# FFT-form 7x7 convolution on one core: a later gate for the pixel loads, an earlier weight difference, DMA lanes in program order, four output buffers

## The chip, the cores and the metric

The kernel runs on one core of a Trainium2 chip. The metric is the device time of one execution in microseconds (us). Each execution is classed fast or slow (slow here: over 1.5% above the fastest of the same kernel), and only fast ones are compared; one execution, of e11, was slow and is left out. The profile's span is about 1.7 us shorter than the device time of the same execution.

## The reference, cut to what matters

```python
def reference(x, w):                 # x: 1x224x224x96 bf16, w: 7x7x96x96 bf16
    wp = jnp.pad(w, ((0, H - K), (0, W - K), (0, 0), (0, 0)))
    Xf = rfft2(x as f32, axes=(1, 2))
    Wf = rfft2(wp as f32, axes=(0, 1))
    Yf = jnp.einsum('bhwi,hwio->bhwo', Xf, Wf)
    return irfft2(Yf, s=(H, W)) as bf16
```

It is a circular 7x7 convolution with 96 input and 96 output channels.

## The kernel before

The kernel transforms only along the height, in blocks of 28 rows plus 6 of overlap. `Fm` is the forward matrix (pixels to frequencies, written to `xf`), `WF` the filters in the frequency domain, made from `wq` by matmuls and, for about a third of the slots, as a difference of two others (`w_sub`). VectorE forms the combined input `J` (42 operations `J<-J` in the run, one per group of frequencies and tile). The products land in PSUM banks (`pb`), become `yf`, and go through a scratch buffer in HBM (`scr`), from which they come back transposed (`tt`) for the inverse matrix `Gm`. Results are cast to `yo` and stored.

The last tile has no later work to hide behind, so it is stored in four parts, `scra` (frequencies 0 to 8) and three `scrb`, loaded back into `xf` buffers that are free by then, and multiplied in two halves, `GA` and `GB`. Between the halves, 16 filler matmuls on zeros (`wu`) are meant to keep TensorE's clock up.

By the instruction listing every DMA takes one of eight semaphores, called lanes here, in turn, in the order in which the scheduler meets it, and waits for the DMA that had the lane last. The traces show DMAs landing on eight semaphores, and the longest wait of one DMA for another on the sync queue of the kernel before is 6.3 us (for `scrb<-yf`).

```python
    gate = []
    def dma(out_ap, in_ap):                      # loads and stores on the sync queue
        r = DE.dma_start(out=out_ap, in_=in_ap)
        if gate:                                 # held until gate[-1] has run
            tc.add_manual_dep(r.ins, gate[-1].ins.name, SYNC, reason="queue order")
        return r
    ...
    for _ in range(3):                           # warm-up: 3 x 8 matmuls on zeros
        pwu = bank()
        for _ in range(8):
            TE.matmul(pwu[:]..., lhsT=wu[:, 0:128], rhs=wur, start=True, stop=True)
    ...
    xgo = sin_q(qf[:])                           # sine table, ScalarE
    ...
    after(xgo, x0_loads)                         # first pixel loads: J edge rows, then xn
    ...
    VE.tensor_copy(out=Fm.rearrange("p r s j -> p j s r"), in_=qf[:])
    ...
    def put_y(t, s):                             # store of a group of rows of yf
            ...
            def put(eng=DE):
                eng.dma_start(out=dst..., in_=yf[...])
            if t == TL and s < NS - 1:           # last tile: on ScalarE's queue
                puts.append(lambda: put(SE))
            else:
                put()
    ...
    yo_pool = ctx.enter_context(tc.tile_pool(name="yo", bufs=3, side="right"))
    ...
            if s == 3:
                queue_c(t - 1)                   # tt loads of the tile before
            ...
            if t == TL and s == SL[2] + 2:
                load_b(0, DE, 1)                 # first scrb load
    ...
    load_b(1, DE, 1)
    load_b(2, DE, 1)
    ...
    order = [(g, q) for h in range(2) for g in range(2) for q in range(4 * h, 4 * h + 4)]
    live = {k: first(*k) for k in order[:8]}     # GA halves
    for _ in range(WARM):                        # 16 fillers
        TE.matmul(live[order[7]]..., lhsT=wu[:, 0:M4], ...)
    for i, (g, q) in enumerate(order):
        second(g, q, live[(g, q)], yo)           # GB halves, cast, store
```

## Time and profile before

| | before |
|---|---|
| time, three executions | 290.65 us median (290.49 to 291.18) |
| profiled span | 288.5 us |
| TensorE, VectorE, ScalarE, GpSimd busy | 92%, 84%, 64%, 30% |
| GB matmuls start, start to end of the run | 279.06, 9.4 us |

In the profile's lines PE is TensorE, PEld its weight loads, DVE VectorE, ACT ScalarE, POOL GpSimd; SPq and ACTq are DMAs issued on the sync queue and on ScalarE's. The granted clock is the share of TensorE's full clock that the chip's throttle let through. From the page of the kernel before: a row of busy tenths of TensorE in 40 equal slices of the span, and the granted clock in tenths of full speed.

```profile
PE   8398898999989889999999999999999999999592
PEclk9869999999979999999999999999999999999867
```

One digit is 7.2 us. TensorE has its gaps in the second slice (the filters are not there yet) and in the last slices. The clock fell to half at 12.3, 80.6 and 271.7 us, for 6.83, 3.41 and 6.83 us, and once more when the work was done (285.4). In this trace all falls and rises are whole multiples of 3.41 us apart; one such step of 3.41 us, between two places of this grid, is called a window below. From the list of waits of the kernel before (what waited for what; us in total, times, longest):

```profile
ACT yo L82 <- DMA out_dram<-yo: 3.2, 1, 3.2
...
PE pb L82 <- ACT yo L82: 2.3, 1, 2.3
DVE yo L82 <- DMA out_dram<-yo: 2.2, 1, 2.2
```

All three stand in the tail near 272 us.

### The profile page before, as it was taken

What the parts mean: (1) busy time and instruction counts of PE and PEld (TensorE: products, weight loads), DVE (VectorE), ACT (ScalarE), POOL (GpSimd) and SP (SyncE); (2) the same over time, 40 slices, a digit from 0 to 9 for tenths busy, and PEclk for the clock granted to TensorE, in tenths of its full rate; (3) what the DMA queues carried; (4) which work ended last, traced back from release to release, by engine and by line L of the source; (5) the groups of instructions that cost most, each with busy time, mean ns of one, the idle gap of its engine ahead of it and who ended that gap; (6) DMA issues with size and microseconds to landing.
All of it is one profiled execution on the core that took longest, in us unless ns stands there. A gap on an engine that the chain in (4) does not pass through costs nothing.

```text
span 288.5 us, 11546 instructions
## 1 busy us (share of the span) xinstructions
PE 266.1 (92%) x4814; PEld 238.4 (83%) x4814; DVE 243.0 (84%) x524; ACT 184.7 (64%) x459; POOL 87.4 (30%) x122
## 2 busy tenths in 40 slices
PE   8398898999989889999999999999999999999592
PEld 3298898999889888888988988898989898889271
DVE  6289999998998999789968899878987789898623
ACT  5089875657413955986888768886688864173313
POOL 2741001234325312521432224223323324426000
PEclk9869999999979999999999999999999999999867
DMA  8667331111211559979688671986749433684955
GB/s 170 132 188 203 83 104 62 45 43 43 85 45 43 168 176 199 284 206 283 166 203 235 180 253 57 228 224 192 250 134 218 150 106 126 181 236 123 222 151 180
DMA packets 44364, 46.01 MB, mean 159 GB/s; under 512 B 33442, under 2 KB 35054, under 8 KB 44216
## 3 DMA queue, kind: packets, MB, share of 16 engines
q1 hardware_dynamic: 43464, 42.90, 55.3%
q10 hardware_dynamic: 848, 2.37, 3.0%
q8 instruction: 38, 0.62, 0.9%
q14 instruction: 14, 0.11, 0.1%
HBM read 23.92 MB, written 21.33 MB: 157 GB/s over the span
## 4 chain that ended last, share of the span: by engine, by line
PE 52%; DVE 29%; DMA 10%; issue 4%; POOL 2%; ACT 1%; DVEq 0%; SPq 0%; POOLq 0%; ACTq 0%
PE pb L82 52%; DVE J L82 9%; DVE v L82 6%; DVE xf L82 5%; DMA wq<-in_w_dram 4%; DVE yf L82 4%; DMA xn<-in_x_dram 4%; DVE WF L82 3%; DVE u L82 2%; DMA out_dram<-yo 2%; POOL yf L82 2%; ACT xf L82 1%; ACT yo L82 0%; DVE tt L82 0%; DVE yo L82 0%
## 5 line engine op out<-in xcount | busy, mean ns | idle before, releaser
L82 PE MATMUL pb<-WF,J 96*128 96x96 bf16 x2898 | 167.6, 207 | 4.4 <-DVE J L82 3.9
L82 PEld LDWEIGHTS <-J 96*128 96x128 bf16 (+1 forms) x2910 | 143.5, 98 | 19.0 <-issue 8.2
L82 POOL TENSOR_TENSOR yf<-v,u 128x384 bf16<-128x384 f32 x75 | 75.3, 1018 | 163.6 <-issue 91.2
L82 ACT CAST xf<-pb 96x408 bf16<-96x408 f32 (+1 forms) x139 | 60.7, 472 | 7.4 <-PE pb L82 4.5
L82 PE MATMUL pb<-WF,xf 96*128 96x96 bf16 x952 | 60.7, 207 | 1.9 <-DVE WF L82 1.8
L82 ACT CAST yo<-pb 84x384 bf16<-84x384 f32 (+1 forms) x130 | 56.1, 481 | 9.4 <-PE pb L82 6.1
L82 DVE TENSOR_TENSOR J<-xf 96x1824 bf16<-96x1824 bf16 (+1 forms) x84 | 57.2, 720 | 0.1
L82 PEld LDWEIGHTS <-xf 96*128 96x128 bf16 x952 | 47.5, 98 | 2.2 <-issue 2.0
L82 PE MATMUL pb<-Fm,xn 118*128 118x136 bf16 x448 | 46.2, 223 | 1.6 <-DVE u L82 0.8
L82 PE MATMUL pb<-tt,Gm 102*84 102x384 bf16 (+1 forms) x144 | 35.7, 329 | 1.3 <-DVE yf L82 0.8
L82 ACT CAST WF<-pb 96x480 bf16<-96x480 f32 (+1 forms) x57 | 29.2, 566 | 9.0 <-PE pb L82 8.8
L82 PEld LDWEIGHTS <-xn 118*128 118x128 bf16 x448 | 30.1, 98 | 2.6 <-issue 1.5
L82 PE MATMUL pb<-wq 98*128 98x120 bf16 (+1 forms) x288 | 24.4, 238 | 4.6 <-DMA xn<-in_x_dram 4.6
L82 PEld LDWEIGHTS <-wq 98*128 98x128 bf16 x288 | 21.5, 151 | 5.2 <-issue 5.2
L82 DVE TENSOR_TENSOR J<-J 96x912 bf16<-96x912 bf16 (+1 forms) x42 | 25.0, 595 | 0.0
L82 DVE TENSOR_TENSOR yf<-v,u 128x384 bf16<-128x384 f32 x36 | 20.5, 571 | 1.2
L82 DVE CAST xf<-pb 96x408 bf16<-96x408 f32 (+1 forms) x33 | 15.5, 506 | 0.7 <-PE pb L82 0.6
L82 PEld LDWEIGHTS <-Gm 102*84 102x84 bf16 (+1 forms) x144 | 11.8, 114 | 4.2 <-issue 1.6
L82 PE MATMUL pb<-wu 128*128 128x512 bf16 (+1 forms) x40 | 12.4, 488 | 1.1 <-DVE ct L82 1.1
L82 DVE CAST WF<-pb 96x480 bf16<-96x480 f32 (+1 forms) x15 | 9.1, 614 | 5.0 <-PE pb L82 4.5
L82 PEld LDWEIGHTS <-wu 128*128 128x128 bf16 (+1 forms) x40 | 6.1, 155 | 6.9 <-issue 2.9
L82 DVE COPY xf<-xf 96x816 bf16<-96x816 bf16 x12 | 9.3, 817 | 0.0
(390 smaller groups left out, 216.4 us busy)
## 6 DMA issues: line engine op xcount, KB each, us to landing
xn<-in_x_dram SPq DMA_DIRECT2D x13, 672.0 KB
scr<-yf SPq DMA_DIRECT2D x30, 288.0 KB
tt<-scr SPq DMA_DIRECT2D x24, 288.0 KB
out_dram<-yo SPq DMA_DIRECT2D x24, 252.0 KB
tt<-scr SPq DMA_DIRECT2D x12, 192.0 KB
out_dram<-yo SPq DMA_DIRECT2D x12, 168.0 KB
scr<-yf SPq DMA_DIRECT2D x6, 192.0 KB
scra<-yf ACTq DMA_DIRECT2D x3, 288.0 KB
```

What stands on the lines that cost most here:

```text
L82: r = fn(*a, **k)
```

## The change

The intent, part by part: (1) the pixel loads wait for the cast of `Fm` instead of the sine, so that the filter loads have the DMA engines alone for longer; (2) eight more warm-up matmuls shorten the hole before the filter matmuls; (3) the first weight difference is made whole in round 0; (4) every DMA is put in program order, so that it takes its lane in that order, and the early stores of the last tile go on the sync queue; (5) four output buffers in place of three; (6) finer cuts of the last stores.

```diff
+    dlast = [None]
+    def dorder(r):
+        if dlast[0] is not None:
+            tc.add_manual_dep(r.ins, dlast[0].ins.name, NOSYNC, reason="program order")
+        dlast[0] = r
+        return r
     def dma(out_ap, in_ap):
 ...
-        return r
+        return dorder(r)
 ...
-    for _ in range(3):
+    for _ in range(4):
         pwu = bank()
 ...
-    xgo = sin_q(qf[:])
+    sin_q(qf[:])
 ...
-    after(xgo, x0_loads)
 ...
-    VE.tensor_copy(out=Fm.rearrange("p r s j -> p j s r"), in_=qf[:])
+    xgo = VE.tensor_copy(out=Fm.rearrange("p r s j -> p j s r"), in_=qf[:])
+    after(xgo, x0_loads)
 ...
-                eng.dma_start(out=..., in_=...)
+                dorder(eng.dma_start(out=..., in_=...))
-            if t == TL and s < NS - 1:
+            if t == TL and SA <= s < NS - 1:
                 puts.append(lambda: put(SE))
 ...                                             (the same dorder() in load_b)
-        add(max(0, 2 * b0 - 10), 2 * b0 - 4 if gi > 1 else 2, ...)
-        ... enumerate(... if gi > 1 else ((0, 0), (1, 0))):
+        add(max(0, 2 * b0 - 10), 2 * b0 - 4 if gi > 1 else 1, ...)
+        ... enumerate(... if gi > 1 else ((0, 0), (0, 0))):
 ...
-                now = wsubs.pop((r, t)) + now if r < 2 else now + wsubs.pop((r, t))
+                now = wsubs.pop((r, t)) + now if r < 1 else now + wsubs.pop((r, t))
 ...
-    yo_pool = ctx.enter_context(tc.tile_pool(name="yo", bufs=3, side="right"))
+    yo_pool = ctx.enter_context(tc.tile_pool(name="yo", bufs=4, side="right"))
 ...
-        cut = (1, 3) if i < 4 or i >= 12 else (3,)
+        cut = (1, 3) if i < 4 else (3,) if i < 12 else (1, 2, 3)
```

More of the change, by code (lines that the diff above doesn't have):

```diff
@@ L569, in put @@
             def put(eng=DE):
-                eng.dma_start(out=dst.rearrange("w j s e -> (w j) s e")[:, y0 - yo0:y1 - yo0],
-                              in_=yf[:, 0:y1 - y0].rearrange("p s r m o -> p s (r m o)"))
-            if t == TL and s < NS - 1:
+                dorder(eng.dma_start(out=dst.rearrange("w j s e -> (w j) s e")[:, y0 - yo0:y1 - yo0],
+                              in_=yf[:, 0:y1 - y0].rearrange("p s r m o -> p s (r m o)")))
+            if t == TL and SA <= s < NS - 1:
                 puts.append(lambda: put(SE))
@@ L599, in load_b @@
             w0, w1 = h * TW // nh, (h + 1) * TW // nh
-            eng.dma_start(out=tl_b[KO[i]:KO[i] + KB[i], w0:w1], in_=sb[:, w0:w1])
+            dorder(eng.dma_start(out=tl_b[KO[i]:KO[i] + KB[i], w0:w1], in_=sb[:, w0:w1]))
     def g_parts():
@@ L715 @@
         b0 = PGRP[gi][0]
-        add(max(0, 2 * b0 - 10), 2 * b0 - 4 if gi > 1 else 2, prep_jobs(gi) if gi > 1 else p1)
-        for h, (r, t) in enumerate(((max(b0 - 4, 2), 1), (b0 - 2, 0)) if gi > 1 else ((0, 0), (1, 0))):
+        add(max(0, 2 * b0 - 10), 2 * b0 - 4 if gi > 1 else 1, prep_jobs(gi) if gi > 1 else p1)
+        for h, (r, t) in enumerate(((max(b0 - 4, 2), 1), (b0 - 2, 0)) if gi > 1 else ((0, 0), (0, 0))):
             wsubs.setdefault((r, t if r >= LAG else 0), []).append(w_sub(gi, h))
@@ L841 @@
             live[order[k]] = first(*order[k])
-        cut = (1, 3) if i < 4 or i >= 12 else (3,)
+        cut = (1, 3) if i < 4 else (3,) if i < 12 else (1, 2, 3)
         if q % 4 in cut:
-            q0 = 0 if q % 4 == cut[0] else cut[0] + 1
+            q0 = max([-1] + [c for c in cut if c < q % 4]) + 1
             w0 = TL * 2 * TW + q // 4 * PXC
```

## The prediction

> **What bounds the kernel now.** I read the page first (TensorE busy 92%, VectorE 84%: no engine is free, so look by stage), then the table of five-microsecond stretches, then the chain that ended last, then the timelines of the two stretches where TensorE is not full: the start and the end. From the table of stretches (busy us of PE, PEld, DVE, ACT, POOL, granted clock, DMA share, GB/s):
>
> ```profile
> 20.00:25.00 5.00, 4.93 (x74) 4.45 (x71) 5.00 (x12) 5.00 (x15) 0.00 (x0) 1.00 0.47 125
> 30.00:35.00 5.00, 4.88 (x89) 4.62 (x88) 5.00 (x11) 4.15 (x11) 0.00 (x0) 1.00 0.19 36
> 35.00:40.00 5.00, 3.78 (x69) 3.55 (x67) 4.96 (x11) 3.66 (x10) 0.00 (x0) 1.00 0.34 114
> ...
> 250.00:255.00 5.00, 5.00 (x103) 4.56 (x100) 4.54 (x11) 2.98 (x9) 1.87 (x2) 1.00 0.77 206
> 270.00:275.00 5.00, 2.66 (x10) 1.64 (x10) 1.46 (x3) 0.85 (x2) 0.00 (x0) 0.67 0.85 222
> ```
>
> From about 18.5 to 50 us VectorE has no hole: it is the bound there, even where TensorE stands still (35 to 40). From about 110 to 266 us TensorE is full. From 267 on nobody is full: that is the tail, bound by waits. The chain through the tail, and the sync queue's timeline there:
>
> ```profile
> 266.20 0.23 ACT tt__7217 L82
> 266.44 6.13 DMA out_dram<-yo
> ...
> 272.64 0.48 ACT yo L82
> ...
> 273.17 9.68 PE pb L82 x41
> ```
>
> ```profile
> 259.39 6.96 SPq L82 DMA_DIRECT2D xf<-scra  x2
> 266.44 0.63 SPq L82 DMA_DIRECT2D out_dram<-yo  x1
> 267.12 0.36 SPq L82 DMA_DIRECT2D xf<-scrb  x1
> 268.62 0.34 SPq L82 DMA_DIRECT2D scrb<-yf  x1
> 272.00 3.04 SPq L82 DMA_DIRECT2D xf<-scrb  x2
> ```
>
> The two loads of the last tile's first part (xf<-scra) should go out together at 259.4; the second goes at 266.03. The queue's waits name the cause:
>
> ```profile
> SPq L82 <- DMA scrb<-yf: 6.3, 1, 6.3
> ```
>
> That second load reads nothing of scrb. The instruction listing shows that it waits for a DMA semaphore lane (there are eight, taken in turn) that a later store on ScalarE's queue holds. The output store behind it is late by the same 6 us, so its yo buffer is late, ScalarE's yo cast waits 3.2 us, TensorE gets no bank (2.3 us), and the 16 filler matmuls start at 274.4. They end only at 278.9, when the second halves (GB) start:
>
> ```profile
> 274.40 4.82 PE L82 MATMUL pb<-wu 128*112 128x384 bf16 x16
> 279.06 0.98 PE L82 MATMUL pb<-xf,GB 128*112 128x384 bf16 x5
> ```
>
> In the start, these matter:
>
> ```profile
> 13.14 4.99 PE L82 MATMUL pb<-wq 98*128 98x100 bf16 x56 [4.56 <-DMA xn<-in_x_dram]
> 36.53 0.33 PE L82 MATMUL pb<-WF,xf 96*128 96x96 bf16 x4 [1.21 <-DVE WF L82]
> ```
>
> The first name is wrong: by the listing these matmuls wait for the six filter loads. The second is the wait that the weight-difference move aims at.
>
> [...] falls and rises at 12.3, 19.1, 80.6, 271.7 and 278.5 us are whole multiples of 3.41 us apart. [...] the fall at 80.6 closes a window with one hole of 1.46 us, that at 271.7 one with nine matmuls in it. [...] the store issued at 268.62 stood behind 432 + 168 + 288 KB of earlier sync-queue work and landed only at about 274.7, when the load that needs it was released. [...] Here a 288 KB store with the queue nearly to itself took 257.08 to 259.36, 2.3 us.
>
> **The change part by part.**
>
> *Pixel loads held to the cast of Fm.* The gate moves from the sine's end (7.24 us) to the cast's end (8.62), 1.4 us later. The small J loads (133 KB) compete less with the filters, but on the engines that finish last (data until 12.0 us) they still queue behind the filter rows. J is needed at 17.9, no earlier. I count 0 to 0.3 us, take 0.1.
>
> *Eight more warm-up matmuls.* At 0.213 us each (spacing of the last ones) they end at 8.58 + 8 x 0.213 = 10.3 instead of 8.6; the hole before the filter matmuls shrinks from 4.5 to 2.8 us. With the holes seen to drop the clock (1.46 us in a window) it still falls in most phases of the window, later. A full clock would remove VectorE's hole between 17.94 and 18.51 and start its first cast some 0.2 us sooner, 0.8 at most; at a chance of a quarter 0.2 us.
>
> *First weight difference whole in round 0.* Eight filter matmuls (two banks) move ahead of the first tile-1 forward matmuls, where TensorE waited 0.7 us for pixels anyway, and the second 0.89 us difference moves up one round. TensorE's 1.21 us wait at 36.5 should go. But VectorE is the bound there and runs the same differences; moving one buys nothing by itself. What does buy: the casts split otherwise. Counting the listing to round 5, VectorE loses a 0.64 us filter cast and a 0.43 us short xf cast and gains one of 0.5: 0.57 us less, ScalarE takes them. So 0.6 us.
>
> *Lanes in program order, early scra stores on the sync queue.* The second scra load goes at 259.8 instead of 266.0, the 56-row output at 260.5, both into a DMA system with idle time (0.0 to 0.1 share from 264 to 267). So the ring is nearly free when the last store goes out at 268.62: I give it 2.4 us, to 271.0, and its load 2.8 us (the same load in the kernel before: issued 274.73, its data through by about 276.5, landed by my estimate at 277.5): GB's data at 273.9, in place of 277.5. TensorE: the twelve tail casts on two engines end at 271.5 (six of 0.49 on VectorE from 268.5), the last first-half matmul at 271.6, then 16 fillers: 2.6 us at full clock (0.163 each), end 274.4; at half clock about 4.3, end 275.9, as the clock comes back within the row. GB starts at 274.4 or 275.9 in place of 278.9: 4.5 or 3.0 us, mean 3.7. Against it: the store of rows 0 to 2 now stands in program order before the tt loads, which start at 247.1 instead of 245.06 (its wait is for GpSimd's yf, end 246.72). The first tile is used at 250.02; with the store's 288 KB ahead in the ring it lands at 250 to 251. TensorE is the bound there: a new wait of 0 to 1 us, take 0.5.
>
> *Four output buffers.* The only waits on yo's stores are the two in the tail (3.2 and 2.2 us). The lane order cures the same wait, so I count nothing extra.
>
> *Last stores cut finer.* One store more of 0.32 us issue, the last one 84 instead of 168 KB; but 688 KB are still to move after 284, at about 290 GB/s. 0.1 us either way: 0.
>
> Sum: 0.1 + 0.2 + 0.6 + 3.7 - 0.5 = 4.1 us. 290.65 - 4.1 = 286.5.
>
> **The rivals.** (a) *The filler takes the DMA's place.* If the clock falls near 271.7 again, the 16 fillers, not the transfer, set GB's start. For it: the tail casts still leave about 1 us of holes in that window. Against: no 2.3 us stop any more. It makes 287.2 instead of 285.7. (b) *The late tt loads stop TensorE at 250.* For it: 2.0 us later issue, 5 us of lead before; against: only the first of six tiles is urgent. At worst 1 us more: 287.5. (c) *The start gives more than I count*: filters land earlier and the clock stays up, VectorE's row starts 1 us sooner; with a full tail gain 284 to 284.5. For it: the author tuned exactly these; against: the DMA engines' late ones are busy with filter rows until 12 us in both. (d) *The start gives nothing*, because another VectorE wait opens behind the doubled difference (it now waits for ScalarE's filter casts): 287.2.
>
> **Range and chances.** Faster by over 2% means under about 284.9: it needs the upper end of both gains. The tail's sum alone is between 2 and 4.7 us, the start's between 0 and 1.6. I predict 286.3 (the sum, a little towards rival c), 283.8 to 288.6; faster 0.2, same 0.79, slower 0.01.
>
> **What would show it.** Right: in the sync queue's timeline both scra loads within 1 us of each other; no yo wait on out_dram; the last scrb load issued about 2.4 us after its store, not 6; the GB matmuls starting about 6 us after that store's issue, in place of 10.3; VectorE without holes from 18 to 50 us, its first combined J at 44.5 coming some 0.6 to 1 us sooner. Wrong: TensorE waiting on tt<-scr near 250 for over 1 us; fillers at 0.3 us each up to the GB matmuls; the filter matmuls starting well before 13.1; or scrb1's store, which shares the engines with scrb0's load, landing later than 270 and holding the queue.

## The result, and the profile after

In four executions each, the changed kernel took 286.35 us (median, 285.81 to 287.81) and the kernel before 290.91 us (290.49 to 291.51): ratio 0.985, 95% interval 0.981 to 0.989, within 2%. Here and below a ratio is the mean time of one kernel's fast runs over that of the other's of the same rounds, so not quite the ratio of the medians that are quoted.

That first reading agrees with the prediction to 0.05 us, better than it deserves. Later (e5), in six executions, the same kernel took 288.41 us (287.14 to 289.36) and the kernel before 290.99: ratio 0.992 (0.989 to 0.995). Over all ten executions the median is 287.5 us, and eight of the ten lie in the predicted range. Much of what the experiments found is about where this spread comes from.

From the page of the changed kernel, the same two rows (7.1 us a digit), in the execution of 285.95 us:

```profile
PE   8599998999979889999999999999999999989982
PEclk9979999999979999999999999999999999999998
```

The gap in the tail is gone and the clock stays up there. Two of its five-microsecond stretches (busy us of PE, PEld, DVE, ACT, POOL, granted clock, DMA share, GB/s), to be laid beside those of the prediction:

```profile
35.00:40.00 5.00, 4.73 (x87) 4.35 (x85) 4.96 (x11) 4.58 (x12) 0.00 (x0) 1.00 0.28 95
...
270.00:275.00 5.00, 3.69 (x21) 2.45 (x21) 0.78 (x2) 0.00 (x0) 0.00 (x0) 1.00 0.72 189
```

At 35 to 40 us TensorE works 4.73 instead of 3.78 us, and VectorE has no hole in either kernel (4.96): the wait has gone, the bound has not moved. At 270 to 275 the clock is 1.00 instead of 0.67. The sync queue's timeline of the changed kernel (start us, us, queue, what):

```profile
245.19 0.35 SPq L82 DMA_DIRECT2D scra<-yf  x1
245.72 4.32 SPq L82 DMA_DIRECT2D tt<-scr  x9
...
259.56 0.99 SPq L82 DMA_DIRECT2D xf<-scra  x2
...
268.03 0.34 SPq L82 DMA_DIRECT2D scrb<-yf  x1
268.55 3.77 SPq L82 DMA_DIRECT2D xf<-scrb  x2
```

Both scra loads go within a microsecond, the lane wait is gone. The last scrb load leaves at the end of the last row, 272.0 us, 4.0 us after its store: the prediction gave the store 2.4. TensorE's timeline of the changed kernel, with the idle time before a group in brackets:

```profile
249.73 0.49 PE L82 MATMUL pb<-tt,Gm 102*84 102x384 bf16 x2 [1.09 <-DMA tt<-scr]
...
271.00 2.76 PE L82 MATMUL pb<-wu 128*112 128x384 bf16 x16
274.79 0.99 PE L82 MATMUL pb<-xf,GB 128*112 128x384 bf16 x5 [1.03 <-issue]
```

The new wait for tt is there (1.09 us). The fillers run at full clock and end at 273.76, and GB then waits another microsecond for the last load: the profile names no releaser here, but the trace's semaphore of that load is complete at 274.70. GB starts 6.8 us after the last store's issue; before it was 10.4.

**A ledger.** To find where the time went I subtracted the start times of the same `J<-J` operation in two profiles. All differences are to the profile of the kernel before, in us; negative is earlier. The first J stands at 27.46 us there, the others at the times in the header, GB at 279.06; the last columns are the time from the last J to GB, and the span.

| profile | 1st J | 37.7 | 181.6 | 253.6 | 258.8 | last J, 263.0 | GB | last J to GB | span |
|---|---|---|---|---|---|---|---|---|---|
| before | 0 | 0 | 0 | 0 | 0 | 0 | 0 | 16.04 | 288.5 |
| changed kernel, first | -0.03 | -0.45 | -0.74 | -1.54 | -1.02 | -0.64 | -4.27 | 12.41 | 284.2 |
| changed kernel, again (e5) | +0.52 | +0.09 | +0.06 | -0.72 | +1.46 | +1.85 | -2.75 | 11.44 | 285.5 |
| head alone (e1) | +0.94 | +0.52 | +0.55 | +0.59 | +0.85 | +1.24 | +1.64 | 16.44 | 290.0 |
| tail alone (e2) | -0.12 | -0.12 | -0.04 | -0.84 | -0.40 | -0.01 | -3.05 | 13.00 | 285.4 |
| four buffers (e3) | +0.25 | +0.25 | +0.34 | -0.45 | -0.45 | -0.07 | -2.38 | 13.73 | 286.2 |
| lanes in order (e4b) | -0.33 | -0.33 | -0.26 | +3.39 | +3.39 | +3.68 | +1.48 | 13.84 | 291.4 |
| lanes and scra stores (e6) | +0.36 | +0.35 | +0.34 | +0.35 | +4.05 | +4.44 | -0.25 | 11.35 | 288.2 |
| tt loads first (e7) | +0.57 | +0.14 | +0.26 | -0.54 | -0.55 | -0.16 | -3.89 | 12.31 | 284.7 |
| six warm-up rows (e8) | -0.02 | -0.44 | -0.43 | -1.24 | -0.76 | -0.37 | -2.74 | 13.67 | 285.3 |

### The profile page after: what moved, and what is told of

It is laid out like the page before. It is cut to its first block, busy times and chain, and to the rows that moved or that the text cites.

```text
span 284.2 us, 11562 instructions
## 1 busy us (share of the span) xinstructions
PE 265.4 (93%) x4822; PEld 237.2 (83%) x4822; DVE 242.0 (85%) x523; ACT 185.6 (65%) x460; POOL 87.6 (31%) x122
## 4 chain that ended last, share of the span: by engine, by line
PE 51%; DVE 29%; DMA 7%; issue 5%; ACT 3%; POOL 3%; DVEq 0%; SPq 0%; POOLq 0%; ACTq 0%
PE pb L82 51%; DVE J L82 10%; DVE v L82 5%; DMA wq<-in_w_dram 4%; DVE xf L82 4%; DVE yf L82 3%; DVE WF L82 3%; POOL yf L82 3%; DVE u L82 2%; ACT xf L82 2%; DMA xn<-in_x_dram 2%; DMA tt<-scr 1%; DVE yo L82 1%; ACT WF L82 0%; DVE tt L82 0%
## 5 line engine op out<-in xcount | busy, mean ns | idle before, releaser
L82 ACT CAST WF<-pb 96x480 bf16<-96x480 f32 (+1 forms) x58 | 29.8, 575 | 8.9 <-PE pb L82 8.7
L82 PE MATMUL pb<-wq 98*128 98x120 bf16 (+1 forms) x288 | 23.8, 232 | 3.5 <-DMA xn<-in_x_dram 3.5
L82 DVE CAST WF<-pb 96x480 bf16<-96x480 f32 (+1 forms) x14 | 8.3, 612 | 5.0 <-PE pb L82 4.9
```

What stands on the lines that cost most here:

```text
L82: r = fn(*a, **k)
```

## The experiments

Twelve runs follow (eleven new kernels, and the changed one again), all with correct results. Each was timed in five rounds beside the kernel before, on the same chip as the others of its group.

### e1: the head alone

Edit: the kernel before with the lines of parts 1 to 3 of the diff above (gate, fourth warm-up row, weight difference), nothing else.

> The kernel before with the head's three parts alone (gate at the cast of Fm, fourth warm-up row, first weight difference whole in round 0). Theory: the combined J operations come 0.4 us sooner from 37 us on (as in the changed kernel), the tail is as before, so 0.4 to 0.7 us less, ratio 0.9975 to 0.9985. Rival: the further 1.1 us that the changed kernel gains between 108 and 240 us belongs to the head's moves too; then 1.0 to 1.6 us less at the J before 254, ratio about 0.995.

Measured: 290.69 us (289.57 to 291.74) against 290.38, ratio 1.0023 (0.9987 to 1.0058). Neither: the head gains nothing by itself. The ledger says why. From the first J to the second it gains the 0.42 us that the weight difference was moved for (+0.94 to +0.52), but the first J itself is 0.94 late. The stretch in which the filter matmuls run (columns as above):

```profile
15.00:20.00 5.00, 5.00 (x57) 5.00 (x56) 3.85 (x8) 3.93 (x8) 2.60 (x7) 0.50 0.97 254
```

The filter matmuls start at 13.81, 0.7 us later than in the kernel before, and run at half clock to the end of this stretch: here the clock came back only at 20.6 us instead of 19.1. The middle of the run does not move (+0.55 at 181.6, +0.59 at 253.6), so the rival that gave the head the gain there falls.

### e2: the tail alone

Edit: the kernel before with parts 4 to 6 of the diff.

> The kernel before with the tail's parts alone (lanes in program order, early scra stores on the sync queue, four output buffers, finer last cuts). Theory: GB starts 3.5 to 4 us sooner; with the tt wait of about 1 us near 250 counted, 3.0 to 3.8 us less in all, ratio 0.987 to 0.990; the J's up to 245 us are where they were. Rival: the four output buffers also free the middle, 108 to 240 us: J's there 0.7 to 1.1 us sooner, ratio 0.983 to 0.986.

Measured: 287.63 us (287.08 to 288.67), ratio 0.992 (0.989 to 0.995); a smaller gain than either expected. GB comes 3.05 us sooner, which looks like the theory's 3.0 to 3.8, but 0.80 us of it is the middle's, between 181.6 and 253.6, where the rival is right; from the last J to GB the gain is 3.04 us where the theory had 3.5 to 4. TensorE's timeline near the tt wait:

```profile
250.36 0.49 PE L82 MATMUL pb<-tt,Gm 102*84 102x384 bf16 x2 [1.02 <-DMA tt<-scr]
```

From 253.6 to 258.8 it costs 0.44 us in the ledger.

### e3: four output buffers alone

```diff
-    yo_pool = ctx.enter_context(tc.tile_pool(name="yo", bufs=3, side="right"))
+    yo_pool = ctx.enter_context(tc.tile_pool(name="yo", bufs=4, side="right"))
```

> The kernel before with four output buffers in place of three, nothing else. Theory: the second scra load still goes at 266, the ring is as late as before and the last scrb load still lands near 277.5, so GB can start at most 1.4 us sooner, though TensorE no longer waits for a yo cast: 0.5 to 1.4 us less, ratio 0.995 to 0.998. Rival 1: the output buffer alone is the gain of the tail, 3 us or more, ratio below 0.990. Rival 2: it is worth nothing, 1.000, because the late out store still holds the cast through its lane. Middle: J's at 108 to 240 us unchanged by the theory, 0.7 sooner by the rival that the mid-run gain is the buffers'.

Measured: 288.02 us (287.23 to 288.94), ratio 0.9936 (0.990 to 0.997). This is more than the theory gave, and less than rival 1. The wait for yo is gone although the lanes are as before; the second scra load still goes late (264.65), the last scrb load at 272.7, and GB starts when it lands:

```profile
271.80 4.07 PE L82 MATMUL pb<-wu 128*112 128x384 bf16 x16
276.68 0.99 PE L82 MATMUL pb<-xf,GB 128*112 128x384 bf16 x5 [0.81 <-DMA xf<-scrb]
```

So most of the tail's gain is to be had by either of two cures of the same wait: from the last J to GB 2.3 us with the buffer alone, 3.0 with the whole tail part.

The middle gain of 0.8 us is in this kernel too, and it is the buffer's: all profiles with four buffers have it, and those with three (e1, e6, and e4b up to 248 us) do not. It does not come from a wait for yo. TensorE's timeline near 210 us, first of the kernel before:

```profile
210.20 0.28 PE L82 MATMUL pb<-Fm,xn 118*128 118x136 bf16 x2
210.68 0.79 PE L82 MATMUL pb<-tt,Gm 102*84 102x384 bf16 x2 [0.19 <-DVE u L82]
```

and of the kernel with four buffers:

```profile
210.16 0.28 PE L82 MATMUL pb<-Fm,xn 118*128 118x136 bf16 x2
210.28 0.67 PE L82 MATMUL pb<-tt,Gm 102*84 102x384 bf16 x2
```

Both programs have the same instructions in the same order on every engine. The instruction listing shows where they differ, and the trace's semaphores agree (the second line above waits for VectorE before, for ScalarE with four buffers): in the engine that a matmul waits for before it may overwrite its PSUM bank. In one such place:

```
before:        pb<-tt,Gm [waits DVE]   pb<-tt,Gm [waits DVE]          pb<-WF,J [waits Activation]
four buffers:  pb<-tt,Gm [waits DVE]   pb<-tt,Gm [waits Activation]   pb<-WF,J [waits DVE]
```

As I read it, the scheduler hands out the banks, and another buffer elsewhere changed its choice; here the new choice waits less. That is a by-product, not a rule, and no run changed the banks alone.

### e4b: lanes in program order alone

Edit: `dorder` in `dma`, `put` and `load_b` as in the diff; the stores of the last tile stay on ScalarE's queue, three buffers.

> The kernel before with DMA lanes in program order only (scra stores stay on ScalarE's queue, three output buffers). Theory: both scra loads go together at about 259.5, no yo wait, the tt wait near 250 is absent since the tt loads are issued at 245 as before: 3.5 to 4.5 us less, ratio 0.985 to 0.988, better than the tail as a whole. Rival: with three output buffers the yo wait stays (2 us or more) and the gain is under 2 us, ratio above 0.993.

Measured: 292.64 us (292.10 to 293.17), ratio 1.0089 (1.006 to 1.012). A miss of both, and of 6 to 7 us for the theory. ScalarE's timeline:

```profile
251.36 0.37 ACTq L82 DMA_DIRECT2D scra<-yf  x1
251.84 0.41 ACT L82 ACTIVATE tt__6652<-pb 128x288 f32<-128x288 f32 x1 [6.93 <-DMA tt<-scr]
```

In program order the first scra store has a lane that a tt load had, and by the listing it waits for it (in the trace that lane is complete at 251.28, and the store goes out at 251.36). But it is issued by ScalarE, and in this trace the wait stands in ScalarE's own stream: ScalarE did nothing for 6.9 us, VectorE waited 3.5 us for it, and TensorE then 2.5. The move of the early scra stores to the sync queue is what makes the order of the lanes usable (ratio 0.9926 in e6, 1.0089 here); the tt wait is the price of that move: 0.44 to 0.52 us where the clock holds (e2, e8, the first profile), against 3.6 between 248 and 253.6 us here.

### e5: the changed kernel again

> The changed kernel again, on the chip of this call, because the head alone (1.0023) and the tail alone (0.992) do not multiply to its 0.985. If the two simply add, it reads 0.991 to 0.995 here; if they need each other, or the first reading stands, 0.983 to 0.988. The filter matmuls' start and the phase of the clock's edges should again differ from its first profile by some tenths of a microsecond, and the first combined J with them.

Measured: 288.41 us (287.14 to 289.36), ratio 0.992 (0.989 to 0.995): the parts simply add (1.0023 times 0.992 is 0.994). In the ledger this profile loses 2.18 us at 253.6 to 258.8, where the first lost 0.52. The stretches there (columns as above):

```profile
249.00:252.00 3.00, 1.86 (x24) 1.45 (x22) 2.53 (x7) 1.26 (x3) 1.95 (x2) 0.78 1.23 207
252.00:255.00 3.00, 3.00 (x45) 2.83 (x43) 2.42 (x5) 1.09 (x3) 0.25 (x1) 0.65 1.31 193
```

and of the first profile of the changed kernel:

```profile
252.00:255.00 3.00, 3.00 (x68) 2.89 (x66) 2.14 (x6) 2.35 (x6) 1.46 (x2) 1.00 1.31 198
```

Both had the same tt wait (1.14 and 1.09 us). In one, the granted clock fell to half from 250.7 to 254.1 us, and TensorE, which is the bound there, ran 45 matmuls where the other ran 68. The falls at 15.2 and 250.7 are 69 times 3.41 us apart, as on the grid of the kernel before. A second hole may count too, a wait for a J some 2 us ahead of the tt wait. TensorE's timeline of this profile, and the same hole in the first one:

```profile
247.85 0.34 PE L82 MATMUL pb<-WF,J 96*128 96x96 bf16 x4 [0.55 <-DVE J L82]
250.60 0.78 PE L82 MATMUL pb<-tt,Gm 102*84 102x384 bf16 x2 [1.14 <-DMA tt<-scr]
```

```profile
247.03 0.34 PE L82 MATMUL pb<-WF,J 96*128 96x96 bf16 x4 [0.53 <-DVE J L82]
```

Counted back from the falls, here both holes lie in the window that closes with the fall (247.25 to 250.67, 1.69 us idle); in the first profile an edge at 247.72 parts them, and 1.09 us remain. In e8 an edge parts them as well (1.06 us) and the clock holds; in e2 an edge cuts through the tt wait, 1.17 us remain in the first window, and it holds; in e6 an edge cuts it too, 1.32 us remain, and it falls. These five profiles fit that where the windows lie decides whether the wait counts; but the two longest waits are also the two that lost the clock, and no run moved the windows on purpose.

### e6: lanes in order and early scra stores on the sync queue, three buffers

```diff
-            if t == TL and s < NS - 1:            # on top of e4b
+            if t == TL and SA <= s < NS - 1:
```

> The kernel before with the lanes in program order and the early scra stores on the sync queue, but three output buffers. Theory: no ACT instruction is held near 245 (that was the scra store waiting for a lane on ScalarE's queue), both scra loads go together at about 260, no yo wait of over 1 us, GB about 6.8 us after the last scrb store; the 0.7 us that the fourth buffer's bank order gives between 188 and 243 us is missing: ratio 0.993 to 0.996. Rival: the yo wait is the three buffers' and comes back with 2 us, ratio 0.998 or more.

Measured: 289.07 us (286.90 to 289.97), ratio 0.9926 (0.989 to 0.997). ScalarE is no longer held, no yo wait of over a microsecond is left, and GB starts 5.7 us after the last store: the lanes cure the wait with three buffers too. The middle gain is missing, as expected (+0.34 at 181.6, +0.35 at 253.6). In this profile the tt wait is 1.29 us, and the clock was then at half for two windows:

```profile
252.00:255.00 3.00, 3.00 (x34) 2.71 (x34) 2.77 (x6) 1.26 (x3) 0.21 (x1) 0.50 1.33 180
255.00:258.00 3.00, 3.00 (x35) 2.71 (x33) 0.70 (x3) 1.26 (x3) 0.99 (x1) 0.50 1.21 208
```

From 253.6 to 258.8 the ledger loses 3.70 us. The six executions fall in two groups, 286.9 and 287.1 at a mean clock of 0.986 and four from 288.9 to 290.0 at 0.966 to 0.974.

### e7: the changed kernel, tt loads ahead of the first scra store

```diff
-            if s == 3:
+            if s == (2 if t == TL else 3):
                 queue_c(t - 1)
```

> The changed kernel, with the last tile's tt loads put ahead of the first scra store in program order. Theory: tt loads issued at about 245.1, TensorE's wait for tt of 1.1 us near 249.7 is gone, the J's from 253 on come 0.5 to 1 us sooner, and 0.5 to 1 us less than the changed kernel in the same rounds. Rival: the scra store waits behind six tt loads, or the tail waits on transfers anyway; 0 to 0.3 us.

Measured: 286.73 us (286.36 to 287.80), ratio 0.9866 (0.984 to 0.989); by the means of six, 1.35 us less than the changed kernel in the same rounds. TensorE's timeline:

```profile
249.88 0.49 PE L82 MATMUL pb<-tt,Gm 102*84 102x384 bf16 x2 [0.24 <-ACT tt__6747 L82]
```

The wait for tt is gone, and from 253.6 to 258.8 the J's lose nothing (-0.54 to -0.55). The gain is larger than the 0.5 us that the wait costs where the clock holds, and the spread fell from 2.2 to 1.4 us; both fit an end of the falls of the clock at 250. That each long execution of the changed kernel is such a fall is not shown: only one execution of a run leaves a trace.

### e8: the changed kernel with six warm-up rows

```diff
-    for _ in range(4):
+    for _ in range(6):
```

> The changed kernel with six warm-up rows in place of four, ending near 13.7 us, so that no hole stands before the filter matmuls. Theory: the clock does not fall before 18 us whatever the window's phase; the 56 filter matmuls take about 2.6 us instead of 4.3 to 5.0, the first combined J comes 0.5 to 1 us sooner than in the changed kernel, and so does the end: 0.3 to 1 us less in the same rounds. Rival: the head is held by the loads of J and xn or by VectorE's own row, and the end moves by under 0.3 us.

Measured: 286.69 us (286.43 to 287.02, five executions), ratio 0.986 (0.983 to 0.989), 1.6 us less than the changed kernel by the means. The same stretch as in e1:

```profile
15.00:20.00 5.00, 4.48 (x74) 4.33 (x73) 4.45 (x9) 4.72 (x11) 2.61 (x7) 1.00 0.99 273
```

The clock was full from the start to 80.1 us. The 56 filter matmuls started at 14.26, after a wait of 0.76 us, and took 3.64 us, not the 2.6 I expected. They start 0.06 us apart from the first one on, before any cast could hold them; the weight loads beside them are as busy as they are (4.33 and 4.48 us in the line above). The first J came 0.54 us sooner than in the changed kernel of the same rounds, but no sooner than in its first profile, where the clock happened to hold until 15.6. That leaves about 1 us of the gain unexplained: the tt wait is still there (1.06 us), and the two profiled executions, 287.02 and 287.23 us, are only 0.2 us apart. Since e8 gains as much as e7 and spreads less (0.6 us), the end of the falls at 250 is not the only way to lose the long executions.

### e9 to e12: the two together, and three attempts on top

e9 has both edits above. e10 is e9 with the last scrb store ahead of the first scrb load. e11 is e9 with the gate back at the sine. e12 is e9 with the small filter loads ahead of the large ones.

```diff
                                                   # e10
-            if t == TL and s == SL[2] + 2:
-                load_b(0, DE, 1)
     tail[0] = 2
+    load_b(0, DE, 1)
     load_b(1, DE, 1)
                                                   # e11
+    xgo = sin_q(qf[:])
+    after(xgo, x0_loads)
-    xgo = VE.tensor_copy(out=Fm..., in_=qf[:])
-    after(xgo, x0_loads)
+    VE.tensor_copy(out=Fm..., in_=qf[:])
                                                   # e12, in load_w: this line moved to the end
     eng.dma_start(out=wq[h * PW:h * PW + 48, 0:n], in_=wsrc[0:48, h * C2:h * C2 + n])
```

> The changed kernel with the tt loads ahead of the first scra store and with six warm-up rows. Theory: the two gains stand at different places (the start, and TensorE's wait at 250 with the fall of the clock that it brings), so they add: 1.5 us less than either alone, about 285.3 us, ratio 0.980 to 0.984, and a spread of under 1.5 us over six runs. Rival: both only remove the same slow outcomes of the clock; then as each alone, 0.986.

e9: 286.55 us (284.10 to 287.46), ratio 0.986 (0.982 to 0.991). The rival's value; the interval just touches the theory's 0.980 to 0.984. The spread is 3.4 us, where the theory had under 1.5. It has no fall of the clock before 270, but TensorE's timeline shows a new wait in the start:

```profile
18.87 0.52 PE L82 MATMUL pb<-Fm,xn 118*128 118x136 bf16 x6 [1.06 <-DMA xn<-in_x_dram]
```

The filters are done sooner and now the pixels are late: by the listing xn is issued only when the first filter load, whose lane it takes, has landed (in the first profile of the changed kernel the load lands at 12.79 us and xn goes at 12.80; with six rows it goes at 13.0 to 13.4).

> The same as the run before, with the last scrb store ahead of the first scrb load in the sync queue. Theory: the store no longer shares the DMA engines with a 288 KB load and lands in 2.4 to 3 us instead of about 4; the last load's data come 0.5 to 1 us sooner, but two loads stand in the ring ahead of it: 0 to 0.8 us less, and with a clock that falls near 271 nothing, since the fillers then end later than the data. Rival: the 288 KB that now wait behind the store cost as much as is won, 0 or 0.5 us more.

e10: 287.04 us (286.23 to 288.84), ratio 0.989 (0.986 to 0.993). The chain of waits at the end:

```profile
268.14 1.95 DMA scrb<-yf
...
270.11 6.29 DMA xf<-scrb
```

The store now takes 1.95 us, against 4.0 behind a load in the changed kernel, so the load ahead of it had slowed it; but the last load then takes 6.3 us, with two loads ahead of it and 672 KB of output stores issued right behind. The DMA engines were full from 270 to 276 us (shares of 1.15, 1.35 and 0.98 in its three stretches of 2 us), and the order only passed the delay on. GB starts at 276.53, 0.6 us later than in e9, and the mean is 1.2 us longer, not clear of the spread: the rival fits, the theory's gain is not seen.

> As the first of these three, but with the pixel loads' gate back at the end of the sine (J issued at 7.26 instead of 8.65 us). In the ten profiles so far the filter matmuls started at 13.1 to 13.9 us with that gate (mean 13.5) and at 13.7 to 14.4 with the gate at the cast (mean 14.0). If the later gate is what delays them, they start near 13.5 here and the end is 0.3 to 0.6 us sooner; if that was chance, start and end are as in the first of these three, within 0.3 us.

e11: 287.26 us (285.10 to 288.27, five fast executions; the slow one took 289.81), ratio 0.989 (0.984 to 0.993). Inconclusive: the filters were there when the warm-up ended (13.81), so the landing of the last can't be read. One landing can: xn goes out when the first filter load has landed, at 12.98 here, against 12.23 to 12.95 in the five other profiles with the old gate and 12.80 to 13.53 in the seven with the new one and the same order of loads. That does not speak for the gate. The first J was 1.36 us late, in a profile where TensorE waited 1.25 us for xn and the clock then fell from 19.2 to 22.6 us.

> The version with both changes (tt loads first, six warm-up rows), and each filter half's two small loads issued ahead of its large one, so that the first pixel load xn waits for the lane of a small load and not of the large one. In the versions with six warm-up rows TensorE finished the filter matmuls near 17.4 and then waited 0.5 to 1.1 us for xn, which was issued only at 13.0 to 13.4, after the large filter load. Theory: xn is issued near 9.5, TensorE's wait for xn near 19 goes, the first combined J comes 0.5 to 0.8 us sooner than at 27.5, and the end by as much: about 286.0, ratio 0.984. Rival: the 672 KB of xn then share the DMA engines with the filter rows, which land 0.5 to 1.5 us later, and the J with them: 0 to 0.7 us more. The wait near 250 stays away by both.

e12: 286.90 us (285.72 to 287.41), ratio 0.9885 (0.985 to 0.992). First the sync queue's timeline, then a line of the list of waits:

```profile
9.43 0.69 SPq L82 DMA_DIRECT2D xn<-in_x_dram  x2
```

```profile
PE pb L82 <- DMA wq<-in_w_dram: 2.2, 1, 2.2
```

The rival holds: xn goes out at 9.4 us, its wait is gone, and the filters are there only at 15.33, 1.1 to 1.5 us later than in e8 and e9; the first J, at 29.05, is 1.5 us later than e9's. In the start the lane wait was doing useful work, as I read it; the edit also puts the large filter loads behind the small ones, and no run separates the two.

## Why the prediction was right or wrong

**The total** was right (286.3 predicted; 286.35 in the first reading, 287.5 over ten executions), and so was the likeliest outcome, a change of under 2%. Part of that is luck: the 0.9 us of the head did not come, which is rival (d)'s outcome by another way, and 0.8 us in the middle came that the prediction had not foreseen. The terms, positive for a gain:

| term | predicted | measured |
|---|---|---|
| gate and warm-ups | 0.1 + 0.2 | -0.5 at the first J (mean of four profiles with both, against five with neither), not separated |
| weight difference | 0.6 | 0.42, in every profile that has it |
| lanes and stores | 3.7 | 3.63 from last J to GB (first profile), 2.0 to 4.7 in the nine others that have both; 2.3 with the buffer and neither (e3) |
| tt wait | -0.5 | -0.44 to -0.52 where the clock holds, -2.2 and -3.7 where it falls |
| four buffers | 0 | 0.8 in the middle, by banks |
| finer cuts | 0 | 0.05 (9.42 to 9.37 us from GB to the end), within the spread of the others |

*Gate and warm-ups.* The step that failed is "I count 0 to 0.3 us": the filter matmuls waited for their loads until 13.1 to 13.9 us in the five profiles with the old gate, and until 13.7 to 14.4 in the six with the new gate and the old order of the filter loads (in e10 the warm-up ended too late to tell). That looks like a loss of half a microsecond, but the two ranges overlap, and e11, meant to settle it, could not and rather speaks against the gate. The cause stays open. Of "a chance of a quarter" for a full clock I can say that no profile with four rows had it; six rows had it in three of five. The head as a whole was to give 0.9 us, a ratio of 0.997; alone it gave 1.002 (0.999 to 1.006).

*Weight difference.* The mechanism was right: TensorE's wait of 1.21 us vanished and bought nothing by itself, since VectorE is full there. The gain is what VectorE lost. From first to second J: 10.27 us in the five profiles without the move, 9.85 in the nine with it, to 0.01. The count of casts gave 0.57, which I rounded up; the term was 0.18 too large. By the trace VectorE loses a filter cast of 0.63 us and a short xf cast of 0.42 between the two J's and gains one of 0.58, not 0.5.

*Lanes.* The size was right in the first profile, the reasons half. The store took 4.0 us, not 2.4, because it shared the engines with a scrb load (ahead of that load it took 1.95, e10); the load behind it took 2.7, where the prediction had 2.8; GB waited for the data (274.70), not for the fillers (273.76), which ran at full clock. Rival (a), fillers at half clock that set GB's start, came true only in part: where the clock fell near 271 the fillers were slow (e8: 4.4 us), but GB still waited 0.61 us after them for the load, which landed at 276.23 (GB at 276.32). Two small slips in the sum don't change it: the line shown has GB at 279.06 before, not 278.9, and 271.6 and 2.6 make 274.2, not 274.4. And the statement "the lane order cures the same wait, so I count nothing extra" holds (e3, e6: either cure works), but the other half of it, that the buffer touches nothing else, failed: the banks moved.

*The tt wait* was mis-sized in its tail. "A new wait of 0 to 1 us" is what TensorE waited (1.0 to 1.3 us in five profiles). I had not followed it to the clock: in two of the five the clock then ran at half for one window (e5) or two (e6), in a stretch where TensorE is the bound. I had seen the fall at 80.6 close a window with one hole of 1.46 us, and used that only for the start. By the prediction's own list a wait for tt of over 1 us was a sign of being wrong, and it came, in a total that was right.

*In the first profile*, the remaining 0.35 us is an accident: one of two VectorE copies between 103.6 and 108.0 us took 1.17 us instead of 1.52, a step that no other profile shows. VectorE's timeline of the kernel before,

```profile
105.29 1.80 DVE L82 COPY xf<-xf 96x816 bf16<-96x816 bf16 x2
```

and of the changed kernel:

```profile
104.88 1.45 DVE L82 COPY xf<-xf 96x816 bf16<-96x816 bf16 x2
```

GpSimd worked beside them in both, and its memset of `GA` took 0.41 us in the profile with the fast copy and 0.18 in the one before. No run here separates a cause. The 0.3 to 0.4 us that every other profile loses against the kernel before ahead of the last J was not pursued either.

The sum for the first profile, -0.45 (second J), +0.06 and -0.35 (to 181.6), -0.80 (to 253.6), +0.52 and +0.38 (to the last J), -3.63 (to GB), -0.05 (to the end), is -4.32, and the spans differ by 4.3 us; it must close, since the pieces follow each other, and says where the time went, not why.

## What to carry to other kernels

A wait of a microsecond in a stretch where TensorE is the bound is to be priced with the fall of the clock that may follow it (1.14 us of wait and 2.18 us lost in e5, 1.29 and 3.70 in e6, but 1.09 and 0.52 in the first profile, where the clock held), and judged on many executions, since one profile shows only one phase of the clock's grid. Here DMA lanes in program order were a cure only once no compute engine issued a store whose lane was still taken (ratio 1.0089 in e4b, 0.9926 in e6); such stores went to the sync queue. Where two cures remove the same wait, run each alone, and look at the instruction listing for what else a buffer count moves.

## What the runs show of the clock and of the lanes

- Near 250 us, windows of 3.41 us with 1.69 and 1.32 us of idle time in two holes ended in a fall of the clock (e5, e6); windows with 1.06 (e8), 1.09 (the first profile of the changed kernel) and 1.17 (e2) did not. The share of idle time does not sort all the windows seen: in the changed kernel a window that ended near 12.2 us held a hole of 1.95 us and kept the clock, and near 271 us windows with 0.3 to 0.4 us idle by the trace lost it (e3, e8, e9, e11). Those held 11 or 12 long matmuls; the windows at full clock there that kept it held 14 or more. No run tests a cause.
- Where the clock fell in the start, it fell at 12.3 (before), 13.7 (e1), 15.2 and 15.6 (changed kernel, e5 and first), 17.8 (e12) and 19.2 us (e11). The unchanged kernel's executions here spread from 288.4 to 292.2 us, 1.3%, at mean clocks of 0.964 to 0.987, though how much of that is the clock was not separated.
- In the kernel before, a load that needed only its own data waited 6.3 us for a store that had its semaphore last, and in e4b a store on ScalarE's queue held that engine for 6.9 us.
- The 192 KB store took 1.95 us ahead of a 288 KB load (e10), 4.0 us behind it (the first profile of the changed kernel).
